# Threshold attention and an ELU feed-forward on one core: held ELUs of two feature-row groups, and a re-ordered early stage

## The chip, the core and the metric

The kernel runs on one core of a Trainium2 chip. Five engines work side by side, each through its own queue in order: TensorE (PE, matmuls, with its weight loads PEld), VectorE (DVE), ScalarE (ACT), GpSimd (POOL) and SyncE (SP, which issues most DMAs). The metric is the device time of one execution in microseconds; lower is better.

## The reference

```python
# attention, batch 8, 8 heads, 576 positions, head size 64, float32
scores = (1/8) * q @ k.T
thresh = max(scores, axis=-1) - tau              # tau = 0.02
attn   = softmax(where(scores >= thresh, scores, -1e9))
x      = (attn @ v), heads side by side          # (8*576, 512)
# feed-forward: 4608 tokens, 512 -> 2048 -> 512
h = x @ w_in
g = where(h > 0, h, exp(min(h, 0)) - 1)          # ELU
out = g @ w_out
```

Everything is float32, outputs included.

## The kernel before

**Attention** goes by pairs of heads: 32 pairs (8 batches of 4), each with four row tiles of 128 queries and a tail of 64. For a tile TensorE computes the scores, VectorE the maximum (`L773`), ScalarE exp of scores less maximum (`L783`), VectorE the mask times exp with its sum (`L787`), VectorE the total and reciprocal (`L545`, `L551`), GpSimd or ScalarE the normalization (`L501`, `L426`). The weights are then turned by 32x32 transposes on VectorE (`L640`) and a round trip through DRAM (`there`), or in part on TensorE, and multiplied by V (`L818`, `L826`). The result is copied to `xt`; the 64 tail tokens of each batch go through DRAM (`xtail`, `L845`) and form a ninth token group.

**Feed-forward** goes by nine groups of 512 tokens. Group 0 is computed plainly. Groups 1 to 8 use a fast matrix scheme with seven products instead of eight. A *first product* (`first_product(g, u)`, `L1444`) makes the hidden values of feature row u (0 to 7) of group g for two halves c of the tokens. ScalarE and VectorE read its banks (`L1458`, `L1466`), ScalarE takes exp into one of three small buffers `ge`, `ge`, `km` (`L1474`), GpSimd or ScalarE subtracts 1 (`L1484`, `L1486`), and VectorE finishes with `min(e - 1, 0) max h`, the ELU (`L1494`). A *second round* multiplies by `w_out`: rounds r = 0 and 1 take feature rows 0 to 3 and 4 to 7. Up to group 6 this is `second_round` (`L1584`). For the last two groups (7 and 8) it is a *deep round*: seven products, some of which are split once more into seven small ones (`deep_product`, matmuls at `L1958`; plain products at `L2020`). A deep round asks VectorE for sums of g into `s_of` before it (`L1864`, `L1866`, queued in `extra` when the second of two feature rows is finished), for second-level sums within it (`kT` and GpSimd's `wTb`, `wTa`, `L1893`), and for adds of what comes out of the banks (`L1970`, `L1980`, `L2026`).

The end of the program runs in this order: first products of group 7, deep round 0 of group 7, first products 0 to 3 of group 8, deep round 1 of group 7, first products 4 to 7 of group 8, deep rounds 0 and 1 of group 8. So the ELUs of the last feature row before a deep round (rows (7,7), (8,3) and (8,7)) aren't needed by that deep round: the one of (7,7) is first read in deep round 1 of group 7, that of (8,3) in deep round 0 of group 8.

**What sets the order.** Three means:

- The early stage (setup, batch 0 and the pairs 4 to 8, group 0 of the feed-forward, the conversion of the weights) is a list of 1270 entries, `EARLY`, written out by hand or by a planner. `follow` walks it: a name is a job (`sc.3` scores of step 3, `su.3` its total, `put.4.2` a copy of turned weights, `rest.7` a weight conversion, `bnorm.5.0.1` a normalization of the pairs, and so on); `:act`, `:dve` or `:pool` picks the engine where it isn't the default; `@f0` picks a bank; `idle17` puts 17 empty transposes on TensorE.
- The steady loop and the end work with an agenda: TensorE's slots advance a clock by a cost, and each piece of work for the other engines is pushed with a due time `at(t, f, key)`; it is issued when the clock passes it. Named shifts move due times: `MOVED` for keys of all even (`s`) or odd (`f`) pairs, `FIRST` for one place.
- `exp(c)` in `first_product` pushes its ELU with a due time; a product that needs it earlier forces all agenda entries up to it. Reusing a `ge` buffer forces the ELU that still reads it. For three feature rows in a set `patient` the due time is 7.0 later once the deep rounds are near:

```python
patient = {(B - 1, 7), (B, 3), (B, 7)}
at(now[0] + (2.0 if c and attending[0] else 1.4)
   + (7.0 if deep_sums and (g, u) in patient else 0.0), lambda: elu(c), f"e{v}{c}")
```

B is 8. All deep and first products together use eight banks in rotation at the end of the program, three at a time.

Of the kernel before, what the change touches and what calls it, by code (L numbers as in the profile page):

```python
# [65 lines left out]
max.1.0 norm.0.0 ld.vd.0.1 prep.q.3.0 first.k.2.0@f0 max.1.1 ld.v.1.1 exp.1.0 th.1.0 rest.1:pool ld.q.3.0
first.t.q.0@f2 exp.1.1 part.0.0@t mask.1.0 th.1.1 add.0 first.k.3.0@f1 prep.k.2.0 mask.1.1 first.t.q.1@f0 ld.v.0.0
su.1:act copy.q.0 sc.2 end.0 norm.0.1:act rec.1 shift.2 prep.k.3.0 norm.1.1 part.0.1@f2 max.2.0 sign.1 idle21@f1
rest.2:pool ld.v.0.1 max.2.1 exp.2.0 th.2.0 ld.vd.0.0 th.2.1 exp.2.1 mask.2.0 add.1 lw.4 put.0.0 mask.2.1 sign.2
norm.1.0 end.1 rest.3 sc.3 ld.v.1.0 su.2:act copy.q.1 add.2 put.0.1 lw.5 part.0.2@t turn.0 max.3.0 part.1.0@f1  # L70
ld.vd.2.1 put.0.2 landed.0 first.q.0.1@f0 max.3.1 exp.3.0 th.3.0 ld.v.3.1 first.q.1.1@f2 part.1.1@t rec.2 ld.v.2.1
th.3.1 exp.3.1 mask.3.0 norm.2.0 ld.vd.1.1 prep.q.0.1 mask.3.1 ld.vd.1.0 put.1.1 part.1.2@f0 turn.1 put.1.0 shift.3
sc.4 end.2 add.3 sign.3 ld.vd.2.0 put.1.2 landed.1 prep.q.1.1 su.3 max.4.0 val.0.block.0@t lw.6 rec.3 max.4.1 exp.4.0
th.4.0 norm.2.1 first.q.2.1@f0 exp.4.1 mask.4.0 th.4.1 part.2.0@f1 norm.3.0 ld.v.2.0 norm.3.1:act idle7@f2 mask.4.1
ld.vd.3.1 put.2.0 end.3 sc.5 su.4:act out.0.block.0 rest.4 shift.4 lw.7 shift.5 sign.4 add.4 ld.v.3.0 max.5.0
part.2.1@t prep.q.2.1 part.2.2@f1 turn.2 val.1.block.0@f2 max.5.1 exp.5.0 th.5.0 rec.4 th.5.1 exp.5.1 mask.5.0
norm.4.0 part.3.0@f0 put.2.2 put.2.1 landed.2 mask.5.1 norm.4.1 part.3.1@f1 put.3.0 part.3.2@t turn.3 rest.5:pool
out.1.block.0 su.5 sc.6 end.4 put.3.1 sign.5 add.5 lw.8 put.3.2 landed.3 max.6.0 val.2.block.0@f0 rest.6 max.6.1
exp.6.0 th.6.0 shift.6 th.6.1 exp.6.1 part.4.0@t mask.6.0 add.6 first.q.3.1@f1 put.4.0 part.4.1@f2 mask.6.1 prep.q.3.1
part.4.2@t turn.4 sign.6 end.5 put.4.2 sc.7 put.4.1 landed.4 rec.5 end.6 lw.9 norm.5.1:act norm.5.0:act  # L80
out.2.block.0:dve val.3.block.0@t su.6 max.7.0 lw.10 max.7.1 th.7.0 exp.7.0 rest.8:pool rec.6 part.5.0@f0
out.3.block.0:dve rest.7 mask.7.0 th.7.1 part.5.1@t norm.6.1 exp.7.1 part.5.2@f1 turn.5 val.0.block.1@f2 shift.8
norm.6.0:act mask.7.1 put.5.0 put.5.2 su.7 sc.8 put.5.1 landed.5 rec.7 shift.7 norm.7.1 sign.8 norm.7.0:act
val.1.block.1@t max.8.0 add.7 max.8.1 exp.8.0 th.8.0 out.0.block.1:dve part.7.0@f0 out.1.block.1 th.8.1 mask.8.0
exp.8.1 add.8 part.6.0@t part.7.1@f1 put.7.0 mask.8.1 part.6.1@f2 sign.7 part.7.2@f0 turn.7 su.8 put.6.0 sc.9 end.7
# [5 lines left out]
norm.10.0 fexp.0.0.0 val.2.block.1@t max.11.0 max.11.1 exp.11.0 th.11.0 fmin.0.0.0 exp.11.1 out.2.block.1:dve
part.10.0@f0 th.11.1 mask.11.0 add.11 part.9.0@t put.10.0 part.9.1@f2 mask.11.1 sign.11 part.10.1@f0 turn.10 shift.12
end.11 sc.12 put.10.1 landed.10 rest.12 shift.13 lw.15 sign.12 su.11:act add.12 half.4@f0 max.12.0 put.9.0 rec.11
max.12.1 exp.12.0 th.12.0 end.12 th.12.1 rest.13 part.9.2@t turn.9 half.5 exp.12.1 mask.12.0 add.13 lw.16 put.9.2
load.q.4 put.9.1 landed.9 mask.12.1 sign.13 sc.13 elu.0.0.0 norm.11.1:act su.12 rec.12 val.0.1@t norm.12.0:act
norm.12.1 max.13.0 end.13 exp.13.0 th.13.0 fexp.0.1.0 mask.13.0 norm.11.0:act fmin.0.1.0 turn.12 su.13:act rest.14
in.0.0:pool sc.14 rest.15 in.0.1:pool rec.13 send.12 in.0.2:pool part.11.0@f1 max.14.0 half.8@f2 in.1.0:pool max.14.1
exp.14.0 th.14.0 elu.0.1.0 th.14.1 lw.17 out.0.1 put.11.0 shift.15 part.11.1@f0 shift.14 exp.14.1 part.11.2@t turn.11
half.2@f1 add.14 mask.14.0 sign.14 put.11.1 mask.14.1 landed.12 norm.13.0:act end.14 sc.15 shift.16 lw.18 put.11.2:dve
landed.11 part.13.0@f0 max.15.0 half.3 max.15.1 exp.15.0 th.15.0 add.15 su.14 sign.15 rec.14 mask.15.0 rest.16 th.15.1  # L100
part.13.1@t turn.13 end.15 exp.15.1 add.16 sc.16 put.13.0 prep.q.4 put.13.1 landed.13 half.9 sign.16 mask.15.1
load.q.5 in.1.1:pool norm.14.1:act max.16.0 in.1.2:pool su.15:act shift.17 val.1.1@t exp.16.0 th.16.0 in.2.0:pool
prep.k.4 fexp.0.0.1 insend.0 rest.18:pool norm.14.0:act mask.16.0 lw.19 rest.17 end.16 fmin.0.0.1:act add.17 su.16
rec.15 lw.20 shift.18 sc.17 out.1.1 rec.16 elu.0.0.1 norm.15.1:act norm.15.0 fexp.0.0.2 part.14.0@t max.17.1 norm.16.0
half.6@f0 put.14.0 max.17.0 in.2.1:pool fmin.0.0.2:act turn.15 exp.17.0 th.17.0 th.17.1 part.14.1@t add.18 sign.17
# [71 lines left out]
def kernel(  # L177
# [13 lines left out]
    B, H, S, D = q.shape  # L191
# [1188 lines left out]
    with tc.manual_schedule():  # L1380
# [748 lines left out]
```

## Time and profile before

| | us |
|---|---|
| median of 3 runs (1269.47 to 1270.43) | 1270.01 |
| the profiled execution | 1268.97 |
| its span, first to last instruction | 1266.9 |

| engine | busy us | share of the span |
|---|---|---|
| PE | 1249.4 | 99% |
| DVE | 1066.1 | 84% |
| POOL | 790.1 | 62% |
| ACT | 584.1 | 46% |

The profile is of one execution, so its sums are made against 1268.97 and not against the median. A timeline row gives start, length, engine, source line, operation, output <- inputs, shape and count, and in brackets idle time in front of it with what ended it. Neighbouring instructions of one line are merged in a row. Lengths overlap by the latency at the end of an instruction, so the distance from start to start is what an instruction costs a busy engine. A row of the chain of waits gives start, length and the engine and line that the end of the program hangs on at that moment; an engine with a q behind its name (SPq) is its sequencer, issuing. The granted TensorE clock was 0.999 in this execution.

### The profile page before, as it was taken

The numbers are of one execution on the slowest core, as the hardware profiler recorded it, in microseconds if no ns is written. First come the engines' busy times: TensorE is split into PE (matmuls) and PEld (weight loads), VectorE is DVE, ScalarE is ACT, GpSimd is POOL, SyncE is SP. The second block draws the span as 40 slices with busy tenths as digits, with TensorE's granted clock in tenths as the row PEclk, the third lists the DMA queues.
The fourth block names the chain that finished last, engine by engine and source line by source line (L and its number), as shares of the span: only waits on it lengthen the run. The fifth ranks groups of instructions, "written<-read, shape, count | busy, mean of one in ns | idle before, by whom it ended". The sixth has DMA issues, their size and how long they took to land.

```text
span 1266.9 us, 22594 instructions
## 1 busy us (share of the span) xinstructions
PE 1249.4 (99%) x7163; PEld 992.5 (78%) x7163; DVE 1066.1 (84%) x2330; ACT 584.1 (46%) x1271; POOL 790.1 (62%) x1144
## 2 busy tenths in 40 slices
PE   7999999999999999999999999999999999999998
PEld 6776576478788887878788878878887888888898
DVE  6998989898889979898889888988989776776776
ACT  6986755453444435352625353443535251434130
POOL 5674544586576747684767657675757474775564
PEclk9999999999999999999999999999999999999999
DMA  9568898998889887988889897988898876334433
GB/s 224 144 177 237 228 260 240 246 299 214 258 205 279 216 245 213 269 238 245 234 226 264 219 267 204 268 214 253 207 279 222 243 217 241 137 125 150 135 112 113
DMA packets 332871, 277.70 MB, mean 219 GB/s; under 512 B 201296, under 2 KB 288336, under 8 KB 332752
## 3 DMA queue, kind: packets, MB, share of 16 engines
q1 hardware_dynamic: 331760, 275.73, 77.9%
q8 instruction: 57, 0.93, 0.3%
q10 hardware_dynamic: 992, 0.53, 0.2%
q14 instruction: 62, 0.51, 0.1%
HBM read 178.85 MB, written 97.32 MB: 218 GB/s over the span
## 4 chain that ended last, share of the span: by engine, by line
PE 79%; DVE 3%; issue 0%; SPq 0%; ACT 0%; DMA 0%; POOL 0%; DVEq 0%; ACTq 0%
PE f L1444 31%; PE f L1584 23%; PE sc L766 8%; PE sc L826 8%; PE f L1958 4%; PE f L2020 2%; PE sc L818 1%; PE sc L813 1%; PE f L953 1%; DVE mx L773 0%; DVE x L640 0%; DVE w_one L787 0%; DMA there<-x 0%; DVE kT L1893 0%; DVE s L1866 0%
## 5 line engine op out<-in xcount | busy, mean ns | idle before, releaser
L773 DVE TENSOR_REDUCE mx<-sc 128x1 f32<-128x576 f32 x252 | 179.9, 750 | 35.5 <-PE sc L766 28.4
L783 ACT ACTIVATE w_one<-sc,mx 128x576 f32<-128x576 f32 x140 | 101.1, 739 | 125.6 <-DVE mx L773 104.5
L779 POOL TENSOR_SCALAR th<-mx,ntau 128x2 f32<-128x2 f32 (+1 forms) x140 | 41.7, 298 | 174.5 <-DVE mx L773 174.4
L766 PE MATMUL sc<-kT,qT 64*128 64x256 f32 (+5 forms) x896 | 126.6, 418 | 2.1 <-ACT xt L432 0.9
L766 PEld LDWEIGHTS sc<-kT,qT 64*128 64x128 f32 x896 | 99.3, 186 | 35.4 <-issue 18.9
L1444 PE MATMUL f<-xt,sw 128*128 128x256 f32 x512 | 123.8, 384 | 0.5 <-ACT xt L432 0.5
L1444 PE MATMUL f<-x,w_in_sb 128*128 128x256 f32 x512 | 122.8, 382 | 0.0
L1444 PE MATMUL f<-xt,w_in_sb 128*128 128x256 f32 x512 | 121.2, 379 | 0.5 <-DVE xt L1053 0.5
L787 DVE SCALAR_TENSOR_TENSOR w_one<-sc,th,w_one 128x576 f32<-128x576 f32 x140 | 109.7, 811 | 13.1 <-ACT w_one L783 12.9
L783 ACT ACTIVATE e<-sc,mx 128x576 f32<-128x576 f32 x112 | 82.7, 742 | 74.5 <-DVE mx L773 72.2
L640 DVE STREAM_TRANSPOSE x<-w_one 128x512 f32<-128x512 f32 (+1 forms) x140 | 100.0, 744 | 15.2 <-POOL w_one L501 10.2
L501 POOL TENSOR_SCALAR w_one<-w_one,rs 128x576 f32<-128x576 f32 x115 | 89.3, 787 | 37.3 <-DVE rs L551 37.3
L1444 PEld LDWEIGHTS f<-xt,sw 128*128 128x128 f32 x512 | 94.1, 190 | 19.5 <-issue 4.3
L1444 PEld LDWEIGHTS f<-x,w_in_sb 128*128 128x128 f32 x512 | 96.2, 190 | 16.1 <-ACT g L1505 3.6
L1444 PEld LDWEIGHTS f<-xt,w_in_sb 128*128 128x128 f32 x512 | 97.2, 190 | 14.0 <-ACT e L783 0.8
L787 DVE SCALAR_TENSOR_TENSOR e<-sc,th,e 128x576 f32<-128x576 f32 x112 | 87.8, 809 | 8.2 <-ACT e L783 7.9
L1584 PE MATMUL f<-w_out_sb,g 128*128 128x256 f32 x384 | 92.0, 382 | 0.0
L1584 PE MATMUL f<-w_out_sb,s 128*128 128x256 f32 x384 | 91.9, 382 | 0.0
L1584 PE MATMUL f<-t,s 128*128 128x256 f32 x384 | 90.7, 379 | 0.0
L501 POOL TENSOR_SCALAR e<-e,rs 128x576 f32<-128x576 f32 x92 | 67.7, 741 | 35.4 <-DVE rs L551 32.6
L1584 PEld LDWEIGHTS f<-w_out_sb,g 128*128 128x128 f32 x384 | 72.0, 190 | 12.2 <-issue 2.9
L1584 PEld LDWEIGHTS f<-w_out_sb,s 128*128 128x128 f32 x384 | 72.0, 190 | 11.8 <-issue 2.5
(344 smaller groups left out, 2902.7 us busy)
## 6 DMA issues: line engine op xcount, KB each, us to landing
there<-x SPq DMA_DIRECT2D x452, 144.0 KB, 3.9
wTb<-there SPq DMA_DIRECT2D x58, 576.0 KB, 6.2
wTa<-there SPq DMA_DIRECT2D x55, 576.0 KB, 4.8
sw<-win_sums SPq DMA_DIRECT2D x62, 384.0 KB, 4.3
t<-wout_sums SPq DMA_DIRECT2D x45, 512.0 KB, 5.2
there<-x SPq DMA_DIRECT2D x112, 80.0 KB, 1.9
wTb<-there SPq DMA_DIRECT2D x56, 160.0 KB, 3.6
wst<-in_moe_w_in_dram SPq DMA_DIRECT2D x16, 512.0 KB, 4.6
```

Source lines behind the costliest of these rows:

```text
L501: nc.gpsimd.tensor_scalar(wv, wv, st["rs"][:, h : h + 1], 1.0, ALU.mult, ALU.mult)
L640: nc.vector.transpose(x[:, :, c0 : c0 + nc_], src.rearrange("p (c g n) -> p g c n", c=nc_, n=T))
L766: on_banks(nc.tensor.matmul(o, qT[r, i * P : (i + 1) * P], kT[r, k0 : k0 + n], start=True, stop=True, skip_group_check=True), o)
L773: on_banks(nc.vector.tensor_reduce(st["mx"][:, h : h + 1], st["sc", h], axis=AX.XY if i == NC else AX.X, op=ALU.max, negate=True), st["sc" ...
L779: nc.gpsimd.tensor_scalar(st["th"][:, cs], st["mx"][:, cs], -1.0, ntau, ALU.mult, ALU.add)
L783: on_banks(nc.scalar.activation(st["e", h], st["sc", h], AF.Exp, bias=st["mx"][:, h : h + 1]), st["sc", h])
L787: on_banks(nc.vector.scalar_tensor_tensor(st["e", h], st["sc", h], st["th"][:, h : h + 1], st["e", h], ALU.is_ge, ALU.mult, accum_out=st[" ...
L826: on_banks(nc.tensor.matmul(o, vm[:, h, c], parts[part][:, g0:g1, h * (NC + 1) + c], start=False, stop=(c == NC - 1), skip_group_check=Tru ...
L1444: nc.tensor.matmul(loc["banks"][place], left[:, j], right[:, j], start=(begins and j == 0), stop=(j == 1), skip_group_check=True)
L1584: nc.tensor.matmul(place(m), lhs, rhs, start=(begins and v == 0), stop=(v == RU - 1), skip_group_check=True)
L1958: nc.tensor.matmul(loc["x"][place][:, :P], left[:, v], right[:, v], start=(begins and v == 0), stop=(v == 1), skip_group_check=True)
L2020: nc.tensor.matmul(loc[c][:, :HM], lefts(g, r, c, m)[:, v], rights(r, m)[:, v], start=(v == 0), stop=(v == RU - 1), skip_group_check=True)
```

## The change

1. **Held ELUs.** `patient` becomes a table of delays: the ELUs of feature rows (7,7) and (8,3) are due 20.0 later instead of 7.0; (8,7) stays at 7.0. In the order that results, the two ELUs (c = 0 and 1) of (7,7), and the four sums of g behind them, leave the middle of deep round 0 of group 7 and stand behind its last adds, among the weight sums (`L1748`) and first adds of group 8's first product. Those of (8,3) leave the middle of deep round 1 and stand at its end and in first product (8,4). Only VectorE's order changes there; those of the other four engines stay.
2. **Early order.** `EARLY` holds the same 1270 entries; some 260 of the jobs stand a few places elsewhere. 24 jobs change engine:

| from, to | jobs |
|---|---|
| DVE to ACT | totals su.0, su.5, su.16, su.19, bsu.4.4, bsu.4.1, bsu.5.4; copy out.2.block.0 |
| ACT to DVE | copy put.4.2 |
| POOL to ACT | rest.0, rest.29, scale.4, bnorm.5.0.1, bnorm.7.2.0 |
| ACT to POOL | rest.7, rest.16, rest.30, rest.31, norm.11.1, bnorm.6.4.0, bnorm.7.1.1 |
| between DVE and POOL | in.4.1 and in.5.2 to POOL, in.4.2 to DVE |

   On ScalarE's queue the first load of K now stands ahead of that of tau. On SP, the xtail stores of some pairs and some fetches stand behind the next send. TensorE's order is unchanged.
3. **Due times.** Nine entries of `MOVED` and one of `FIRST`. In the steady loop this gives VectorE swaps of neighbours (a bank read `L1466` before or after an ELU), the tail's transposes after two of four maxima instead of after all four, and the turn of the next K (`L440`) ahead of the fourth maximum; ScalarE moves a bank copy (`L1506`) behind an exp, GpSimd an add ahead of a subtraction. In pair 9 the fetch of tile 0 is issued 3.6 earlier.

```diff
 FIRST = {
-    "9:3.0": 0.61, "9:turn4": 2.44, ...
+    "9:3.0": 0.61, "9:fetch0": -3.6, "9:turn4": 2.44, ...
 MOVED = {
-    "f20.1": 2.47, "f26.1": 0.42, "f5.1": 4.32, "fout1": 0.83,
-    "s21.0": 0.22, "sexp11": -0.09, "sfetch4": 0.31, "sprep1": -0.32, "sturn4": -1.49,
+    "f20.1": 3.18, "f26.1": -0.14, "f5.1": 3.93, "fout1": 0.47,
+    "s21.0": 0.51, "sexp11": -0.16, "sfetch4": -0.76, "sprep1": -2.36, "sturn4": -3.1,
...
 EARLY = """
-ld.tail.1.0 ld.tau.0.0:act ld.k.0.1 ld.k.0.0:act idle17@f0 ld.q.0.0 ld.k.1.0 ld.k.1.1 lw.0 lw.1 tau first.t.k.0@f0
+ld.tail.1.0 ld.k.0.0:act ld.k.0.1 ld.tau.0.0:act idle17@f0 ld.q.0.0 ld.k.1.1 ld.k.1.0 lw.0 lw.1 first.t.k.0@f0
...
-put.7.1 end.8 lw.11 rest.9 half.0@f1 rec.8 load.k.4 shift.9 put.6.1 max.9.0 add.9 norm.8.1:act put.7.2:dve landed.7
...
+half.0@f1 shift.9 load.k.4 put.6.0 rec.8 max.9.0 add.9 norm.8.1:act put.7.2:dve landed.7 exp.9.0 max.9.1 part.6.2@t
...
-        patient = {(B - 1, 7), (B, 3), (B, 7)}
+        patient = {(B - 1, 7): 20.0, (B, 3): 20.0, (B, 7): 7.0}
...
-                at(now[0] + (2.0 if c and attending[0] else 1.4) + (7.0 if deep_sums and (g, u) in patient else 0.0), lambda: elu(c), f"e{v}{c}")
+                at(now[0] + (2.0 if c and attending[0] else 1.4) + (patient.get((g, u), 0.0) if deep_sums else 0.0), lambda: elu(c), f"e{v}{c}")
```

More of the change, by code (lines that the diff above doesn't have):

```diff
@@ L66 @@
[L66 to L85, printed above, removed]
@@ L91 @@
[L91 to L105, printed above, removed]
@@ new lines @@
+ld.v.0.1 exp.2.0 th.2.0 rest.2:pool ld.vd.0.0 exp.2.1 mask.2.0 th.2.1 add.1 put.0.0 lw.4 mask.2.1 sign.2 rest.3
+norm.1.0 sc.3 end.1 ld.v.1.0 su.2:act copy.q.1 put.0.1 add.2 part.0.2@t turn.0 lw.5 max.3.0 part.1.0@f1 put.0.2
+landed.0 ld.vd.2.1 first.q.0.1@f0 max.3.1 exp.3.0 ld.v.3.1 first.q.1.1@f2 th.3.0 rec.2 part.1.1@t th.3.1 exp.3.1
+ld.v.2.1 mask.3.0 norm.2.0 ld.vd.1.1 prep.q.0.1 mask.3.1 put.1.1 ld.vd.1.0 part.1.2@f0 turn.1 put.1.0 shift.3 sc.4
+end.2 add.3 sign.3 ld.vd.2.0 put.1.2 landed.1 prep.q.1.1 su.3 val.0.block.0@t max.4.0 lw.6 rec.3 max.4.1 exp.4.0
@@ new lines @@
+th.4.0 norm.2.1 first.q.2.1@f0 exp.4.1 mask.4.0 part.2.0@f1 th.4.1 norm.3.0 idle7@f2 ld.vd.3.1 norm.3.1:act mask.4.1
+ld.v.2.0 put.2.0 end.3 sc.5 su.4:act out.0.block.0 rest.4 shift.4 lw.7 shift.5 sign.4 add.4 ld.v.3.0 part.2.1@t
+max.5.0 prep.q.2.1 part.2.2@f1 turn.2 val.1.block.0@f2 max.5.1 exp.5.0 th.5.0 rec.4 th.5.1 exp.5.1 mask.5.0 norm.4.0
+part.3.0@f0 put.2.2 put.2.1 landed.2 mask.5.1 part.3.1@f1 norm.4.1 put.3.0 part.3.2@t turn.3 end.4 out.1.block.0
+rest.5:pool sc.6 su.5:act put.3.1 sign.5 lw.8 add.5 val.2.block.0@f0 max.6.0 put.3.2 landed.3 rest.6 max.6.1 shift.6
@@ new lines @@
+exp.6.0 th.6.0 part.4.0@t rec.5 th.6.1 exp.6.1 mask.6.0 first.q.3.1@f1 add.6 part.4.1@f2 put.4.0 mask.6.1 prep.q.3.1
+part.4.2@t turn.4 sign.6 end.5 sc.7 put.4.1 put.4.2:dve landed.4 lw.9 end.6 norm.5.1:act val.3.block.0@t max.7.0
+out.2.block.0 lw.10 norm.5.0:act su.6 max.7.1 th.7.0 exp.7.0 part.5.0@f0 out.3.block.0:dve th.7.1 exp.7.1 mask.7.0
+rest.7:pool part.5.1@t part.5.2@f1 turn.5 val.0.block.1@f2 rec.6 mask.7.1 norm.6.1 norm.6.0:act put.5.0 shift.8
+rest.8:pool put.5.2 sc.8 su.7 put.5.1 landed.5 rec.7 shift.7 sign.8 add.7 val.1.block.1@t norm.7.0:act max.8.0 max.8.1
@@ new lines @@
+half.1 exp.10.0 th.10.0 rec.9 put.8.0 put.8.2 lw.13 put.8.1 mask.10.0 norm.9.0 landed.8 end.10 norm.9.1 su.10:act
+first.t.q.3@f2 first.t.q.2@f0 sc.11 copy.q.2 copy.q.3 shift.11 rest.11 lw.14 rec.10 val.2.block.1@t fexp.0.0.0
+norm.10.0 max.11.0 max.11.1 exp.11.0 th.11.0 fmin.0.0.0 part.10.0@f0 out.2.block.1:dve exp.11.1 mask.11.0 th.11.1
+part.9.0@t add.11 put.10.0 part.9.1@f2 mask.11.1 sign.11 part.10.1@f0 turn.10 shift.12 sc.12 put.10.1 landed.10 end.11
+rest.12 shift.13 sign.12 lw.15 add.12 half.4@f0 max.12.0 su.11:act put.9.0 max.12.1 exp.12.0 th.12.0 rec.11 end.12
@@ new lines @@
+th.12.1 rest.13 part.9.2@t turn.9 half.5 mask.12.0 exp.12.1 lw.16 add.13 load.q.4 put.9.2 put.9.1 landed.9 mask.12.1
+sign.13 sc.13 elu.0.0.0 norm.11.1 su.12 val.0.1@t rec.12 max.13.0 norm.12.0:act norm.12.1 end.13 exp.13.0 th.13.0
+fexp.0.1.0 mask.13.0 norm.11.0:act fmin.0.1.0 turn.12 su.13:act rest.14 in.0.0:pool sc.14 rest.15 in.0.1:pool rec.13
+send.12 part.11.0@f1 max.14.0 in.0.2:pool half.8@f2 max.14.1 in.1.0:pool exp.14.0 elu.0.1.0 th.14.0 th.14.1 lw.17
+out.0.1 put.11.0 shift.15 part.11.1@f0 shift.14 exp.14.1 part.11.2@t turn.11 half.2@f1 add.14 mask.14.0 sign.14
@@ new lines @@
+put.17.1 sign.21 part.19.1@t turn.19 in.5.0 add.22 part.17.2@f1 turn.17 half.12@f2 put.19.1 landed.19 end.21 put.17.2
+landed.17 in.5.1 in.5.2:pool val.3.1@t shift.23 insend.5 sign.23 insend.4 rest.23 lw.25 sign.22 add.23 copy.k.4:act
+end.22 prep.k.5 rest.24:pool lw.26 out.3.1 t tail.4 half.19 bmax.4.4.0 insend.2 shift.24 bexp.4.4.0 bth.4.4 add.24
+sign.24 bmask.4.4.0 idle3@f1 end.23 bsu.4.4:act wsc.4.0.0 brec.4.4 end.24 lw.27 bnorm.4.4.0:act wsc.4.0.1 insend.3
+shift.25 rest.25 lw.28 bmax.4.0.0 half.16@f1 insend.1 bmax.4.0.1 bexp.4.0.0 load.q.6 bturn.4.4 bth.4.0 sign.25
```

147 lines of the change are left out of this document (76 added, 71 removed), and 18 rows, old and new, of the table MOVED.

## The prediction

> **What bounds the kernel now.** I read the page's busy line first, then the windows, then TensorE's timeline where a window shows it short of full, and last VectorE's and GpSimd's timelines beside those places.
>
> ```profile
> PE 1249.4 (99%) x7163; PEld 992.5 (78%) x7163; DVE 1066.1 (84%) x2330; ACT 584.1 (46%) x1271; POOL 790.1 (62%) x1144
> ```
>
> ```profile
> 0.00:40.00 40.00, 33.59 (x252) 25.61 (x253) 28.28 (x68) 30.20 (x63) 23.64 (x50) 1.00 0.87 205
> 40.00:80.00 40.00, 38.97 (x329) 30.78 (x328) 36.79 (x89) 38.14 (x79) 25.43 (x37) 1.00 0.56 150
> ...
> 440.00:480.00 40.00, 40.00 (x227) 32.31 (x226) 32.64 (x72) 15.78 (x35) 19.97 (x32) 1.00 0.89 248
> ...
> 1120.19:1143.40 23.21, 21.93 (x161) 20.44 (x160) 19.02 (x42) 5.02 (x15) 16.44 (x17) 1.00 0.34 114
> 1217.18:1238.38 21.20, 21.20 (x162) 20.30 (x160) 16.15 (x41) 5.03 (x15) 11.90 (x14) 1.00 0.42 141
> ```
>
> In a window row, the columns behind the length are busy time of TensorE, its weight loads, VectorE, ScalarE and GpSimd. TensorE is the bound: 1249.4 us of 1266.9. In the steady loop (440 to 480) it is busy 40.00 of 40, so nothing that changes there can save time; it can only lose some. What can be won lies where TensorE stands still: in the early stage (the first two rows) and in the deep rounds. The last two rows are the first and the third deep round, group 7 round 0 and group 8 round 0. They issue the same slots of matmuls, yet the one takes 23.21 us and the other 21.20, without a gap. The first loses 2.01 us to waits.
>
> **Deep round 0 of group 7.** The four gaps in TensorE's timeline, and two rows of the chain of waits that give the undisturbed pace (0.44 to 0.45 us for four 128x128 instructions, so 0.89 for eight, 1.73 for eight 128x256):
>
> ```profile
> 1131.62 0.61 PE L1958 MATMUL f<-t,g 128*128 128x128 f32 x4
> 1133.23 1.16 PE L1958 MATMUL f<-x,kT 128*128 128x128 f32 x8 [1.00 <-DVE kT L1893]
> 1134.23 1.89 PE L2020 MATMUL f<-w_out_sb,s 128*128 128x256 f32 x8
> 1136.16 0.68 PE L1958 MATMUL f<-x,wTb 128*128 128x128 f32 x4
> ...
> 1139.80 0.61 PE L1958 MATMUL f<-w_out_sb,s 128*128 128x128 f32 x4
> 1140.65 1.13 PE L1958 MATMUL f<-w_one,kT 128*128 128x128 f32 x8 [0.24 <-issue]
> ```
>
> ```profile
> 1189.65 1.73 PE f L2020 x8
> 1191.38 0.44 PE f L1958 x4
> ```
>
> Start to start, less the pace: 1131.62 to 1133.23 is 1.61 - 0.45 = 1.16 lost; then 1.00 - 0.89 = 0.11; 1.93 - 1.73 = 0.20; and 1139.80 to 1140.65 is 0.85 - 0.45 = 0.40. Together 1.87 of the 2.01. The largest ends on VectorE's kT (the second-level sums, L1893). What VectorE did before it:
>
> ```profile
> 1128.52 1.64 DVE L1494 SCALAR_TENSOR_TENSOR wTb<-km,wTb 128x512 f32<-128x512 f32 x1
> ...
> 1130.60 0.97 DVE L1866 TENSOR_TENSOR s<-wTb 128x256 f32<-128x256 f32 x1
> 1131.49 0.41 DVE L1893 TENSOR_TENSOR kT<-g 128x256 f32<-128x256 f32 x1
> 1131.83 0.41 DVE L1864 TENSOR_TENSOR e<-s,wTb 128x256 f32<-128x256 f32 x1
> 1132.16 0.68 DVE L1494 SCALAR_TENSOR_TENSOR wTa<-ge,wTa 128x512 f32<-128x512 f32 x1
> 1132.77 0.41 DVE L1893 TENSOR_TENSOR kT<-kT,g 128x256 f32<-128x256 f32 x1
> ...
> 1133.70 0.94 DVE L1866 TENSOR_TENSOR qm<-wTa 128x256 f32<-128x256 f32 x1
> ...
> 1134.97 0.55 DVE L1864 TENSOR_TENSOR e<-qm,wTa 128x256 f32<-128x256 f32 x1
> ```
>
> The two L1494 rows are the held ELUs, the L1866 and L1864 rows the sums of g that follow them. The change takes all six out of the round and leaves the rest of VectorE's order as it is. Ahead of the end of kT that is 1.64 + 0.89 + 0.34 + 0.61 (start to start from the second on) = 3.48 us; kT was complete at 1132.77 + 0.41 = 1133.18, and would be at about 1129.7. TensorE wants it at 1131.62 + 0.45 = 1132.07. The gap of 1.16 closes, and 0.11 and 0.20 with it, since VectorE then has no backlog (0.94 and 0.55 more go behind it). I don't count the 0.40: by VectorE's rows around it the sum in front of TensorE is held up there by other things than the backlog. Taken: 1.47; ends: 0 and 2.01.
>
> What speaks against it is GpSimd, which runs two long sums at the same time:
>
> ```profile
> 1128.34 2.95 POOL L1051 TENSOR_TENSOR x<-xt 128x512 f32<-128x512 f32 x2
> ```
>
> The ELU that starts inside this row takes 1.64, the one at 1132.16, outside it, 0.68. So 0.96 of the first ELU is a wait on GpSimd, and the kT sums that move up may inherit it. At worst the first kT sum runs only between GpSimd's two sums and the second after 1128.34 + 2.95 = 1131.29, hence ready at 1131.29 + 0.41 = 1131.70, still 0.37 ahead of 1132.07. The Trainium skill (SBUF — State Buffer, Who interferes with whom) says that a VectorE instruction with both inputs in SBUF and a GpSimd instruction that reads SBUF take a shared port in turns, each for its whole length. By that rule the 0.96 is not removed with the ELU but passes to the next such VectorE instruction, which is kT; passed on in full to TensorE it would leave 3.0 - 0.96 = 2.0 us of the sum below, 1268.0. The trace agrees with it in 1.64 against 0.68, and rival (b) has its chance from there.
>
> **Deep round 1 of group 7**, where the ELUs of group 8's first four feature rows go out:
>
> ```profile
> 1180.35 0.61 PE L1958 MATMUL f<-t,wTb 128*128 128x128 f32 x4
> 1181.53 1.16 PE L1958 MATMUL f<-x,kT 128*128 128x128 f32 x8 [0.57 <-DVE kT L1893]
> 1182.52 1.89 PE L2020 MATMUL f<-w_out_sb,qm 128*128 128x256 f32 x8
> 1184.57 0.68 PE L1958 MATMUL f<-x,wTb 128*128 128x128 f32 x4 [0.15 <-POOL ot L1906]
> 1185.09 1.89 PE L2020 MATMUL f<-t,vm 128*128 128x256 f32 x8
> ```
>
> ```profile
> 1177.24 0.68 DVE L1494 SCALAR_TENSOR_TENSOR g<-ge,g 128x512 f32<-128x512 f32 x1
> ...
> 1178.37 0.96 DVE L1866 TENSOR_TENSOR s<-g 128x256 f32<-128x256 f32 x1
> ...
> 1180.12 0.41 DVE L1864 TENSOR_TENSOR s<-s,g 128x256 f32<-128x256 f32 x1
> 1180.46 0.68 DVE L1494 SCALAR_TENSOR_TENSOR g<-km,g 128x512 f32<-128x512 f32 x1
> ```
>
> Lost: 1.18 - 0.45 = 0.73, 0.99 - 0.89 = 0.10, 2.05 - 1.73 = 0.32, 0.52 - 0.45 = 0.07; 1.22 together. The four rows ahead of the kT sum come to 0.68 + 0.96 + 0.41 + 0.68 = 2.73, more than any of the gaps. The 0.32 ends on GpSimd's ot, which adds up what VectorE wrote, and goes with it. Taken: 1.22; ends: 0 and 1.22.
>
> **What the six instructions cost where they go.** They now stand at the head of the next four first products:
>
> ```profile
> 1150.47 0.42 DVE L1466 TENSOR_TENSOR g<-f,t 128x256 f32<-128x256 f32 x1 [1.42 <-POOL t L1463]
> ...
> 1198.79 0.42 DVE L1466 TENSOR_TENSOR wTb<-f,t 128x256 f32<-128x256 f32 x1 [3.56 <-POOL t L1463]
> ```
>
> At the undisturbed durations they are 2 x 0.68 + 4 x 0.41 = 3.00 us, at round 0's 5.19. VectorE idles 1.42 and 3.56 us there. Behind them queue the remaining reads of the deep round's banks, the weight sums (L1748), then the first add. The first add of group 8 may come up to 3.8 us late. ScalarE's exp and GpSimd's minus wait for it, TensorE does not: its eight banks go round in more than two products of three banks, each 28 instructions of 256 columns or 3.5 x 1.73 = 6.1 us long, and nobody reads the g in question before the next deep round (gaps near 1180 above; 1217.18 for the second group). Cost taken: 0; if that cover were gone, up to 3.8.
>
> **The steady loop.** Besides swaps of neighbours, the turn of the next K (L440) goes ahead of the fourth maximum in 11 pairs:
>
> ```profile
> 449.29 0.77 DVE L440 STREAM_TRANSPOSE kT<-qm 128x576 f32<-128x576 f32 x1
> ...
> 451.27 0.81 DVE L787 SCALAR_TENSOR_TENSOR w_one<-sc,th,w_one 128x576 f32<-128x576 f32 x1
> ...
> 456.73 0.45 PE L813 MATMUL sc<-kT,qT 64*64 64x288 f32 x1
> ```
>
> The maximum, its exp and so the last mask can come 0.77 later; the mask ends at 452.08, TensorE needs the banks at 456.73: 4.65 us of cover. Cost 0; without cover 0.77 in each of 11 pairs, 8.5 us.
>
> **The early order.** TensorE's own order is the same instruction for instruction; the 24 jobs that change engine and the others that move shift only who feeds it. Seven totals go from VectorE to ScalarE, and SP issues one send ahead of an xtail store (its issue is in the chain of waits):
>
> ```profile
> 13.67 0.15 DVE L545 TENSOR_REDUCE su<-sm 128x2 f32<-128x4 f32 x1
> ```
>
> ```profile
> 17.35 0.30 ACT L512 ACTIVATE su<-sm 128x2 f32<-128x2 f32 x1 [0.56 <-DVE w L537]
> ```
>
> ```profile
> 230.06 0.44 SPq L845
> ```
>
> Best: 7 x 0.15 + 0.44 = 1.5 us won, all on the path. Worst: 7 x 0.30 = 2.1 us lost, all on ScalarE, which is busy 38.14 of 40 in the second window. I take 0.3 won: nearer to the middle, on the side of the better end, because in that window ScalarE gives up a normalization, a conversion and a small copy and gets one total and one copy.
>
> **Sum.** 1.47 + 1.22 + 0.3 + 0 + 0 = 3.0 us. The profiled execution took 1268.97 (span 1266.9 and 2.07 around it) and would take 1266.0. The median of the runs is 1270.01, 1.04 above it, so the forecast for it is 1267.0.
>
> **Rivals.**
> (a) The early order pays in full and the 0.40 and the rest of round 0 go too: 2.01 + 1.22 + 1.5 = 4.7 won, 1265.3. For it: round 2 of the trace runs without a gap even with its ELUs inside. Against: every early term would have to lie on the path.
> (b) The kT sums of round 0 take over the whole wait on GpSimd, and TensorE still stops near 1133: round 1's 1.22 alone, 1268.8. For it: 0.96 of the ELU is that wait already. Against: 0.37 us to spare at the worst alternation.
> (c) The early order loses its 2.1 on ScalarE: 2.7 - 2.1 = 0.6 won, 1269.4.
> (d) Slower: the turn of K ahead of the fourth maximum delays the tail scores in all 11 pairs: 8.5 - 3.0 = 5.5 lost, 1275.5. It decides once the last mask is later by more than 4.65 us; the shift is 0.77.
> That the ELUs come back into the round by a forced read is excluded: in the new order they stand behind the round's last sums.
>
> **How the numbers follow.** Forecast 0.55, (a) 0.13, (b) 0.22, (c) 0.06, (d) 0.04. Under 0.2%, 2.5 us, a measurement of this kernel can hardly tell from no change. Of the forecast's 0.55 I put 0.44 beyond 2.5 us; with (a) faster is 0.57. The other 0.11, (b) and five sixths of (c) are within: 0.38. (d) and the rest: 0.05. The range, 1265.2 to 1269.4, reaches from (a) to (c) and leaves out (d) and the ends.
>
> **What would show it.** Right: the window from the first L2020 of group 7 to the next L1444 falls from 23.21 to 21.2 to 21.8, no TensorE row there with a gap ending on kT; round 1 without the 0.73; both held ELUs at about 0.7 us behind it. Wrong: a gap of about 1 us still in front of f<-x,kT (b); a TensorE busy time below 40.00 in a steady window (d); a later first L2020 than 1120.19 by over a microsecond (c).

## Result and the profile after

| | before | after |
|---|---|---|
| median (6 runs each) | 1269.71 us | 1265.07 us |
| lowest to highest | 1269.14 to 1270.43 | 1264.75 to 1266.22 |
| profiled execution | 1268.97 | 1265.16 |
| its span | 1266.9 | 1263.4 |

The ratio is 0.9966, with a 95% interval of 0.9955 to 0.9978: 2.8 to 5.7 us faster, 4.6 by the medians. The forecast was 1267.0. The measured median lies 0.1 below the range's lower end of 1265.2.

The busy line and the windows of after. The last two windows are deep rounds 0 and 1 of group 7, from the first L2020 to the next L1444.

```profile
PE 1247.3 (99%) x7163; PEld 992.0 (79%) x7163; DVE 1067.8 (85%) x2322; ACT 584.5 (46%) x1276; POOL 787.2 (62%) x1147
```

```profile
0.00:40.00 40.00, 33.88 (x256) 25.76 (x258) 29.98 (x71) 32.51 (x68) 23.50 (x49) 1.00 0.80 208
40.00:80.00 40.00, 39.27 (x332) 31.02 (x333) 36.68 (x86) 35.94 (x75) 27.50 (x39) 1.00 0.59 156
...
1119.46:1140.68 21.22, 21.22 (x162) 20.39 (x161) 15.40 (x36) 5.03 (x15) 15.05 (x17) 1.00 0.37 125
1166.19:1187.72 21.53, 21.53 (x150) 20.29 (x149) 19.18 (x50) 1.15 (x2) 13.47 (x17) 1.00 0.31 99
```

Round 0 fell from 23.21 to 21.22 us and round 1 from 22.74 (1168.92 to 1191.66) to 21.53. TensorE is busy in all of both. That is 1.99 + 1.21 = 3.2 us. VectorE has 3.6 us less to do in the window of round 0, 15.40 in place of 19.02. Round 0 in TensorE's timeline of after:

```profile
1130.89 0.61 PE L1958 MATMUL f<-t,g 128*128 128x128 f32 x4
1131.34 1.06 PE L1958 MATMUL f<-x,kT 128*128 128x128 f32 x8
1132.23 1.89 PE L2020 MATMUL f<-w_out_sb,s 128*128 128x256 f32 x8
1133.96 0.61 PE L1958 MATMUL f<-x,wTb 128*128 128x128 f32 x4
...
1137.53 0.61 PE L1958 MATMUL f<-w_out_sb,s 128*128 128x128 f32 x4
1137.98 1.07 PE L1958 MATMUL f<-w_one,kT 128*128 128x128 f32 x8
```

From row to row it is 0.45, 0.89, 1.73 and 0.45 us, the undisturbed pace in every case. All four gaps are gone, the one of 0.40 too that the prediction did not count. VectorE in after, and GpSimd's long sums beside it:

```profile
1128.35 0.29 DVE L1980 TENSOR_TENSOR ot<-f,wTb 128x128 f32<-128x128 f32 x1
1128.56 0.59 DVE L1893 TENSOR_TENSOR kT<-g 128x256 f32<-128x256 f32 x1
1129.26 1.30 DVE L1893 TENSOR_TENSOR kT<-kT,g 128x256 f32<-128x256 f32 x1
...
1135.94 0.47 DVE L1893 TENSOR_TENSOR kT<-s 128x256 f32<-128x256 f32 x1
1136.52 1.31 DVE L1893 TENSOR_TENSOR kT<-kT,s 128x256 f32<-128x256 f32 x1
...
1141.51 0.68 DVE L1494 SCALAR_TENSOR_TENSOR wTb<-km,wTb 128x512 f32<-128x512 f32 x1
...
1142.45 0.68 DVE L1494 SCALAR_TENSOR_TENSOR wTa<-ge,wTa 128x512 f32<-128x512 f32 x1
```

```profile
1127.60 2.67 POOL L1051 TENSOR_TENSOR x<-xt 128x512 f32<-128x512 f32 x2
```

The held ELUs run behind the round at 0.68 each. The kT sums moved up to where the ELUs were and took over their wait on GpSimd: 0.59 and 1.30 in place of 0.41 each. The second is ready at 1130.56, 0.78 us before TensorE wants it (1131.34).

The rest of the difference lies elsewhere. TensorE's 7163 matmuls stand in the same order in both kernels, so the start of each can be compared with that of the same matmul. This table gives by how many us each kernel's TensorE is later than the profiled before (minus: ahead), at points named by the time in before. All rows but the first are kernels told of below.

| | 34 | 157 | 950 | 1101 | last matmul |
|---|---|---|---|---|---|
| after | -1.16 | -1.51 | -1.76 | -0.73 | -3.95 |
| after, second trace | -0.57 | -0.89 | -1.11 | -0.89 | -4.11 |
| early order alone | -0.83 | -1.13 | -1.41 | -1.32 | -1.33 |
| held ELUs alone | -0.10 | 0.47 | 0.62 | 0.64 | -2.58 |
| due times alone | -0.01 | -0.39 | -0.29 | -0.10 | 0.22 |
| early order and held ELUs | -1.16 | -1.46 | -1.74 | -1.66 | -4.88 |
| the same, second trace | -0.44 | -0.76 | -1.05 | -0.98 | -4.21 |

After is ahead by 1.2 us at 34 already, and by 1.8 before 950. Of that it loses 1.0 between 950 and 990, all of it in front of this row of TensorE's timeline of after; before has no idle time there:

```profile
961.40 1.99 PE L1444 MATMUL f<-xt,sw 128*128 128x256 f32 x8 [0.81 <-DMA sw<-win_sums]
```

The lead at 34 begins with the first load of K. The rows of TensorE and of ScalarE's queue in before, and then in after, where tau's load is issued behind that of K:

```profile
1.46 3.89 PE L554 MATMUL f<-ident 128*128 128x128 f32 x17 [1.46 <-POOL ident masks.py:199]
5.28 0.37 PE L405 MATMUL f<-ident,w_out_sb 64*128 64x64 f32 x1
6.03 0.63 PE L554 MATMUL f<-ident,w_out_sb 128*128 128x128 f32 x4 [0.38 <-DMA w_out_sb<-in_k_dram]
...
12.73 1.24 PE L493 MATMUL sc<-x 64*128 64x288 f32 x8 [0.69 <-DVE w L537]
...
19.00 0.66 PE L554 MATMUL f<-ident,w 128*128 128x128 f32 x4 [0.40 <-ACT w L426]
```

```profile
0.74 0.40 ACTq L1125 DMA_DIRECT2D tau_sb<-in_tau_dram  x1
1.19 0.44 ACTq L1125 DMA_DIRECT2D w_out_sb<-in_k_dram  x1
```

```profile
1.46 3.55 PE L554 MATMUL f<-ident 128*128 128x128 f32 x17 [1.46 <-POOL ident masks.py:199]
4.94 0.27 PE L405 MATMUL f<-ident,w_out_sb 64*128 64x64 f32 x1
5.17 0.63 PE L554 MATMUL f<-ident,w_out_sb 128*128 128x128 f32 x4
...
10.87 0.76 PE L554 MATMUL f<-ident 128*128 128x128 f32 x5 [0.46 <-ACT qT L426]
...
11.72 1.24 PE L493 MATMUL sc<-x 64*128 64x288 f32 x8
```

```profile
0.74 0.45 ACTq L1125 DMA_DIRECT2D w_out_sb<-in_k_dram  x1
```

K is issued 0.45 us earlier, and the matmul that waited for it starts 0.86 earlier. Of this 0.34 is not the load: the 17 empty transposes in front are done in 3.55 us in place of 3.89. Their single length falls from 0.42 to 0.27 us within the start, in this execution sooner than in that of before; in the second trace of after the transposes take 3.89 again, and it is 0.46 ahead at that matmul.

The wait on VectorE's w in front of the matmul at 12.73 is gone too, but nearly all of it stands just ahead instead, as a wait on ScalarE's qT (the row at 10.87): the two together bring 0.14 us. The largest step of the other moves is at 19.00 of before, where the wait of 0.40 on ScalarE's w is gone (the same matmul starts at 17.49 in after): 0.64 us together with the row behind it. Of that 0.4 us is lost again in front of the scores at 31.70. From 8 us of before on, when the effect of the start is over, all five traces with the early order gain 0.84 to 0.91 us more up to 950, about a third of it by 34 and a third between 34 and 157. In the three traces with the early order that start as slowly as before (the second of after, the second of the two parts together, the early order alone) the lead at 950 is 1.05 to 1.41 us.

### The profile page after: what moved, and what is told of

It is laid out like the page before. It is cut to its first block, busy times and chain, and to the rows that moved or that the text cites. A ratio compares the mean times of both kernels' runs of the same rounds, so it can differ in the third digit from the quotient of the medians.

```text
span 1263.4 us, 22606 instructions
## 1 busy us (share of the span) xinstructions
PE 1247.3 (99%) x7163; PEld 992.0 (79%) x7163; DVE 1067.8 (85%) x2322; ACT 584.5 (46%) x1276; POOL 787.2 (62%) x1147
## 4 chain that ended last, share of the span: by engine, by line
PE 90%; DVE 4%; DMA 2%; ACT 2%; issue 1%; SPq 0%; POOL 0%; DVEq 0%; ACTq 0%; POOLq 0%
PE f L1444 30%; PE f L1584 23%; PE sc L766 9%; PE sc L826 9%; PE f L1958 4%; PE f L2020 3%; PE f L953 2%; PE f L913 2%; PE sc L493 2%; PE sc L818 1%; PE sc L813 1%; DVE mx L773 1%; PE f L554 1%; PE sc L712 1%; PE f L885 1%
## 5 line engine op out<-in xcount | busy, mean ns | idle before, releaser
L779 POOL TENSOR_SCALAR th<-mx,ntau 128x2 f32<-128x2 f32 (+1 forms) x140 | 46.0, 329 | 189.9 <-DVE mx L773 189.8
L1444 PE MATMUL f<-xt,sw 128*128 128x256 f32 x512 | 123.7, 384 | 1.3 <-DMA sw<-win_sums 0.8
L1444 PE MATMUL f<-x,w_in_sb 128*128 128x256 f32 x512 | 122.8, 382 | 0.0
L1444 PE MATMUL f<-xt,w_in_sb 128*128 128x256 f32 x512 | 121.2, 379 | 0.5 <-DVE xt L1053 0.5
L1444 PEld LDWEIGHTS f<-xt,sw 128*128 128x128 f32 x512 | 94.1, 190 | 20.2 <-issue 4.3
L1444 PEld LDWEIGHTS f<-x,w_in_sb 128*128 128x128 f32 x512 | 96.2, 190 | 16.1 <-ACT g L1505 3.6
L1444 PEld LDWEIGHTS f<-xt,w_in_sb 128*128 128x128 f32 x512 | 97.2, 190 | 14.0 <-ACT e L783 0.8
L1584 PEld LDWEIGHTS f<-t,s 128*128 128x128 f32 x384 | 73.0, 190 | 9.9
```

What stands on the lines that cost most here:

```text
L779: nc.gpsimd.tensor_scalar(st["th"][:, cs], st["mx"][:, cs], -1.0, ntau, ALU.mult, ALU.add)
L1444: nc.tensor.matmul(loc["banks"][place], left[:, j], right[:, j], start=(begins and j == 0), stop=(j == 1), skip_group_check=True)
L1584: nc.tensor.matmul(place(m), lhs, rhs, start=(begins and v == 0), stop=(v == RU - 1), skip_group_check=True)
```

## Experiments

**One part at a time.** Each of the first three is the kernel before with one part of the change; the fourth has two.

```diff
# held ELUs alone
-        patient = {(B - 1, 7), (B, 3), (B, 7)}
+        patient = {(B - 1, 7): 20.0, (B, 3): 20.0, (B, 7): 7.0}
# early order alone: EARLY of after, all else of before
# due times alone: MOVED and FIRST of after, all else of before
# early order and held ELUs: MOVED and FIRST of before, all else of after
```

> The kernel before with the held ELUs alone: (7,7) and (8,3) due 20.0 later, the early order and the due times as before. Theory (the three parts of the change work each for itself): the two traces place 1.99 us of the gain in deep round 0 of group 7 (23.21 to 21.22) and 1.21 in deep round 1 (22.74 to 21.53), so about 3.2 us faster than before, and TensorE has no gap in either round. Rival (the sizes of the prediction): 2.7, with the 0.40 us in front of f<-w_one,kT still there. Rival (the waits of the rounds depend on how the earlier stages leave the engines): less than 2, with some of the gaps in the trace.

> The kernel before with the early order alone. Theory: matched matmul by matmul, TensorE in the changed kernel is 1.35 us ahead by 118 us and keeps that to 600, so 1.35 us faster, with the gaps of the two deep rounds as before (1.2 us in front of f<-x,kT in round 0). Rival (the prediction's term): 0.3 us faster. Rival (TensorE's lead is used up at the next common wait): nothing at the end although the lead is there at 118 us.

> The kernel before with the ten due times alone. Theory A (the load of the sums of w_in is issued late enough to be missed): TensorE waits about 0.8 us for sw near 961 us, as in the changed kernel's trace, and the time is 0.3 to 0.8 us longer than before. Theory B (that wait was one execution's DMA and not the order): no such row, and the time is the same within 0.3 us.

> The early order and the held ELUs together, the due times as before: the changed kernel without its third part. Theory (parts add up): 3.2 + 1.35 = 4.5 us faster than before. If the due times cost the 0.8 us of the wait for sw, this beats the changed kernel by 0.5 to 0.8 us; if they cost nothing, it equals it within 0.3 us; if they gain the 0.3 us by which TensorE's lead grew between 118 and 622 us, it is that much slower.

| beside before at 1269.36 | median | by the medians | ratio, 95% |
|---|---|---|---|
| held ELUs alone | 1266.01 | -3.35 | 0.9974 (0.9963 to 0.9984) |
| early order alone | 1267.70 | -1.66 | 0.9987 (0.9978 to 0.9996) |
| due times alone | 1269.88 | +0.52 | 1.0002 (0.9993 to 1.0011) |
| early order and held ELUs | 1264.12 | -5.24 | 0.9957 (0.9945 to 0.9970) |

Rounds 0 and 1 with the held ELUs alone:

```profile
1120.83:1142.04 21.21, 21.21 (x161) 20.38 (x160) 15.42 (x36) 5.03 (x15) 15.09 (x17) 1.00 0.38 125
1167.56:1189.08 21.52, 21.52 (x149) 20.28 (x148) 19.20 (x50) 1.15 (x2) 13.47 (x17) 1.00 0.31 99
```

They are what they are in after, 2.00 and 1.22 us shorter than before, without the other two parts. So the held ELUs give 3.2 us, whatever the early stage does. The early order alone keeps its lead to the end (-1.33 in the table): nothing later uses it up. The parts add up, 3.35 + 1.66 = 5.0 against 5.24. The due times, the third part, bring nothing; whether they cost something was the next question.

**After and the version without its due times, side by side.**

> The changed kernel once more, beside the kernel without its due times on the same chip. If the 0.81 us that TensorE waited for sw at 960.6 us belongs to the order of the change, its trace shows that row again and it stays 0.6 to 0.9 us behind the kernel without the due times. If it was a transfer that landed late in one execution, the row is gone and the two kernels are within 0.4 us of each other.

> The early order and the held ELUs without the due times, once more, beside the changed kernel on the same chip. If the due times cost something in every execution: 0.6 to 0.9 us faster than the changed kernel. If they do nothing: the same within 0.4 us.

On one chip, after took 1264.99 us (0.9965 of before, 0.9953 to 0.9978) and the version without the due times 1264.31 (0.9958, 0.9945 to 0.9972). The second trace of after has no wait for sw: the row at 961 stands there without idle time, so the 0.81 us was a transfer that landed late in one execution. Neither does the trace of the due times alone have it, while that of a kernel without them (30 in place of 20, below) loses 0.23 in front of the same matmul. What comes back in these two traces with the due times is small: 0.2 us at the scores at 973 us, where the three traces of the early order without them lose 0.07 to 0.09 and the first trace of after, where the wait for sw had delayed TensorE before, loses nothing. Over both chips the ten runs without the due times have a median of 1264.19 (1263.77 to 1265.14) and the eleven runs of after 1264.99 (1264.64 to 1266.22). The kernel without the third part is thus the fastest of all, by 0.7 to 0.8 us by the medians; its ratio's interval overlaps that of after. The place at 973 accounts for 0.1 of it. Where the rest comes from, and whether late landings have a part in it, was not settled.

**What in the early order pays.** Two single edits to the kernel before:

```diff
# the first load of K ahead of tau
-ld.tail.1.0 ld.tau.0.0:act ld.k.0.1 ld.k.0.0:act idle17@f0
+ld.tail.1.0 ld.k.0.0:act ld.k.0.1 ld.tau.0.0:act idle17@f0
# the seven totals on ScalarE: su.0 -> su.0:act, and likewise
# su.5, su.16, su.19, bsu.4.4, bsu.4.1, bsu.5.4
```

> The kernel before with one edit in the early order: on ScalarE's queue the first load of K ahead of that of tau. Theory A (the start is bound by the landing of the first K): TensorE passes 6.03 us of before 0.45 to 0.86 earlier, since the load's issue moves up by 0.45 us (1.19 to 0.74), and what is left at 118 us is between 0.25 and 0.86; time 0.3 to 0.9 us shorter. Theory B (the lead is lost in the next wait on VectorE's w, because tau comes later or VectorE is the bound there): nothing left at 20 us, same time.

> The kernel before with another single edit in the early order: the seven totals su.0, su.5, su.16, su.19, bsu.4.4, bsu.4.1 and bsu.5.4 on ScalarE in place of VectorE. Prediction's price: between 7 x 0.15 = 1.05 us faster and 7 x 0.30 = 2.1 slower. Theory A (VectorE's queue is what TensorE waits for early): 0.3 to 1.05 faster. Theory B (only the order of the jobs pays, not the engine): the same within 0.3 us. Rival (ScalarE is the bound between 40 and 80 us): slower by 0.3 or more.

Beside before at 1269.29, the load of K alone gave 1268.69 (0.9994, 0.9985 to 1.0003) and the totals alone 1269.12 (0.9999, 0.9990 to 1.0008). TensorE with the load of K alone:

```profile
5.34 0.66 PE L554 MATMUL f<-ident,w_out_sb 128*128 128x128 f32 x4
...
11.96 1.24 PE L493 MATMUL sc<-x 64*128 64x288 f32 x8 [0.69 <-DVE w L537]
```

The matmul at 6.03 starts 0.69 us earlier (0.15 of it by the transposes: 5.13 in place of 5.28 for the one in front), and TensorE is 0.60 ahead at the last matmul. The time agrees, -0.6, though its interval holds no change. The waits of 0.69 on w at 11.96 and of 0.40 on ScalarE's w, now at 18.23, stay: those go by other moves of the early order. By the runs the seven totals do nothing that can be measured. Their profiled execution was the slowest of that kernel, 1270.87, and 1.7 us late at the matmul that stands at 9.02 in before, ahead of the first of the totals. Of that 0.96 us stands in this row, which takes 1.24 in the others:

```profile
8.64 2.20 PE L493 MATMUL sc<-x 64*128 64x288 f32 x8
```

From there on the matched matmuls can still be compared. The trace with the totals loses another 0.39 us in front of the scores that stand at 31.70 in before, where VectorE's mask waits for GpSimd's w. The five traces with the early order, which has the same seven totals, lose 0.39 to 0.41 there, and none of the traces without them loses anything. So at that place the totals cost, and the gain of the early order comes in spite of them. In the medians (-0.17) this can't be seen.

**Where the held work comes from and where it lands.** Four variants of the kernel before:

```diff
# (7,7) alone
+        patient = {(B - 1, 7): 20.0, (B, 3): 7.0, (B, 7): 7.0}
# all three
+        patient = {(B - 1, 7): 20.0, (B, 3): 20.0, (B, 7): 20.0}
# 30 in place of 20
+        patient = {(B - 1, 7): 30.0, (B, 3): 30.0, (B, 7): 7.0}
# sums of x later; patient as in before
-                    at(clock[0] + 2.99 * k + 8.0, f, f"x{k}")
+                    at(clock[0] + 2.99 * k + 13.0, f, f"x{k}")
```

> The kernel before with only the ELUs of (7,7) due 20.0 later; those of (8,3) and (8,7) stay at 7.0. Theory (each round's waits come from its own held ELUs): round 0 of group 7 takes 21.2 us in place of 23.21, round 1 keeps its 22.74 with the gaps of 0.73 and 0.32; 2.0 us faster than before. Rival (round 1's gaps follow from round 0's): round 1 falls too, 3.2 us faster.

> All three delays at 20.0: the ELUs of (8,7) too leave deep round 0 of group 8, which has no gap to close, and by the order stand with their four sums right ahead of the kT sums of the last round. There kT is ready at 1241.10 and wanted at 1241.89 in the trace of before, 0.79 to spare; the six instructions are 2 x 0.60 + 4 x 0.34 = 2.6 us start to start. Theory (what counts is where the held work lands, and its cover there): 2.6 - 0.8 = 1.8 us slower than with (7,7) and (8,3) alone, so about 1.4 faster than before. Rival (VectorE idles 0.98 us just ahead and takes them up there): at most 0.8 us slower than with the two alone.

> The kernel before with the sums of x for the last group (L1051 and the rows behind it) due 5.0 later, so that GpSimd's two long sums no longer lie beside the held ELUs, which stay in the round. Theory A (0.96 us of the first ELU's 1.64 is a wait on GpSimd): that ELU takes about 0.7, kT is ready 0.96 earlier and the gap of 1.16 in front of f<-x,kT shrinks to about 0.2; up to 1.0 us faster than before, less what the sums cost in their new place. Theory B (the wait is VectorE's own, the backlog alone): the ELU still takes 1.6 and the gap stays at about 1.16; same time.

> The kernel before with the ELUs of (7,7) and (8,3) due 30.0 later in place of 20.0: they stand further on among the first products of group 8. Theory (the first products have cover for them, nobody reads these g before the next deep round): as with 20.0, 3.2 to 3.5 us faster than before. Rival (the reads of the banks that queue behind them hold TensorE up): slower than with 20.0 by 0.5 or more, with a TensorE gap in a first product of group 8.

| beside before at 1269.10 | median | by the medians | ratio, 95% |
|---|---|---|---|
| (7,7) alone | 1267.10 | -2.00 | 0.9983 (0.9974 to 0.9992) |
| all three | 1268.56 | -0.54 | 0.9996 (0.9987 to 1.0005) |
| 30 in place of 20 | 1266.40 | -2.70 | 0.9977 (0.9969 to 0.9986) |
| sums of x later | 1269.08 | -0.02 | 0.9998 (0.9989 to 1.0007) |

With (7,7) alone round 0 gives its 2.0 us and round 1 keeps its gaps:

```profile
1179.58 1.16 PE L1958 MATMUL f<-x,kT 128*128 128x128 f32 x8 [0.57 <-DVE kT L1893]
...
1182.62 0.68 PE L1958 MATMUL f<-x,wTb 128*128 128x128 f32 x4 [0.15 <-POOL ot L1906]
```

So each round's waits come from its own held ELUs.

With all three held, nearly the whole gain is gone. First TensorE at the start of the last round, then VectorE, then GpSimd, at the same time:

```profile
1238.96 0.61 PE L1958 MATMUL f<-t,e 128*128 128x128 f32 x4
1241.38 1.13 PE L1958 MATMUL f<-x,kT 128*128 128x128 f32 x8 [1.81 <-issue]
```

```profile
1236.18 0.85 DVE L1494 SCALAR_TENSOR_TENSOR wTb<-ge,wTb 128x512 f32<-128x512 f32 x1
1236.95 0.68 DVE L1494 SCALAR_TENSOR_TENSOR wTa<-ge,wTa 128x512 f32<-128x512 f32 x1
1237.55 1.49 DVE L1866 TENSOR_TENSOR s<-wTb 128x256 f32<-128x256 f32 x1
1239.07 0.42 DVE L1864 TENSOR_TENSOR e<-s,wTb 128x256 f32<-128x256 f32 x1
...
1240.86 0.42 DVE L1893 TENSOR_TENSOR kT<-kT,e 128x256 f32<-128x256 f32 x1
```

```profile
1237.11 1.65 POOL L1876 TENSOR_TENSOR vm<-wTb 128x512 f32<-128x512 f32 x1 [0.63 <-DVE wTb L1494]
```

The label "issue" must not mislead: kT ends at 1241.28 and the matmul that reads it begins 0.1 later. From 1238.96 it is 2.42 to the next row, 1.97 more than the pace. Expected was a loss of 1.8; by the medians, each against its own before, it is 2.8 worse than with two held; matched matmul by matmul it loses 2.5 there (2.94 ahead before the last round, 0.44 at the end). The price came out higher since one sum behind the ELUs took 1.49 in place of 0.41: it lasted until GpSimd's sum beside it had ended. Six instructions that cost nothing in front of a first product cost 2.5 us in front of a kT sum.

With 30 in place of 20 the window of the first products that take up the ELUs of (8,3) is full:

```profile
1188.58:1214.09 25.51, 25.51 (x126) 22.62 (x125) 17.05 (x30) 10.44 (x26) 15.74 (x19) 1.00 0.43 134
```

The cover is there. By the medians, each against its own before, this kernel is 0.65 us behind the one with 20, on the rival's side of the 0.5; but the intervals overlap, and the rival's mechanism is not there: matched matmul by matmul 0.2 us is lost in round 1 and 0.3 in deep round 0 of group 8, nothing in a first product. The trace of the due times alone, with the ELUs due as before, loses 0.3 in that round too, so the second loss need not come from the 30.

With the sums of x later and the ELUs left in the round, first VectorE, then TensorE, then GpSimd:

```profile
1128.76 0.68 DVE L1494 SCALAR_TENSOR_TENSOR wTb<-km,wTb 128x512 f32<-128x512 f32 x1
...
1131.49 0.42 DVE L1893 TENSOR_TENSOR kT<-kT,g 128x256 f32<-128x256 f32 x1
...
1134.16 1.48 DVE L1893 TENSOR_TENSOR kT<-vm 128x256 f32<-128x256 f32 x1
```

```profile
1131.86 0.61 PE L1958 MATMUL f<-t,g 128*128 128x128 f32 x4
1132.31 1.06 PE L1958 MATMUL f<-x,kT 128*128 128x128 f32 x8
1133.20 1.89 PE L2020 MATMUL f<-w_out_sb,s 128*128 128x256 f32 x8
1135.94 0.68 PE L1958 MATMUL f<-x,wTb 128*128 128x128 f32 x4 [0.85 <-POOL x L1051]
```

```profile
1133.92 1.44 POOL L1051 TENSOR_TENSOR x<-xt 128x512 f32<-128x512 f32 x1
```

The ELU takes 0.68 in place of 1.64, and the gap of 1.16 is not 0.2 but gone, with four of the six instructions still ahead of kT's end: the wait on GpSimd was the part that made the gap. But the sum stands in front of GpSimd's next work and holds VectorE's next kT for 1.48, and 2.74 - 1.73 = 1.01 us of a gap opens there. Most of the wait was moved, not removed: the round takes 22.30 us in this trace (1120.43 to 1142.73), 0.91 less than before, against 2.0 less with the ELUs held, and 0.2 of that is lost again in deep round 0 of group 8. The runs show nothing of the remaining 0.7: by the medians the time is the same, and the interval reaches from 1.4 us faster to 0.9 slower. Theory A is thus right on the ELU and the gap, and what the change is worth in time stays open. With the ELUs held kT still waits for GpSimd, but there is slack in front of TensorE.

## Why the prediction was right, and where it was off

The sign and the main mechanism were right; the size was 3.0 of 4.6. What came about is close to rival (a), 4.7 us and 1265.3, which had a chance of 0.13: round 0 in full, and the early order paying far more than the 0.3 taken. But (a) made its 1.5 us for the early order of the totals, which bring nothing by the medians, and of one issue on SP, which was not tested alone; that its size comes near the measured one is luck.

- **Round 0, 1.47: mis-sized by the gap left out.** The chain (four of the six instructions less in front of kT's end, ready well before it is wanted) held; measured 1.99 to 2.01. The step that failed is that the 0.40 in front of `f<-w_one,kT` was "held up there by other things than the backlog". VectorE's rows of before in front of it:

```profile
1138.03 0.28 DVE L1980 TENSOR_TENSOR wTb<-f,wTb 128x128 f32<-128x128 f32 x1
1138.23 0.91 DVE L1893 TENSOR_TENSOR kT<-s 128x256 f32<-128x256 f32 x1
1139.25 1.30 DVE L1893 TENSOR_TENSOR kT<-kT,s 128x256 f32<-128x256 f32 x1
```

  There is no idle time before 1138.23: VectorE was still working off the backlog. In after the same pair starts at 1135.94, waits as long on GpSimd (1.31), and is ready at 1137.83 for a matmul at 1137.98. The last row does wait on GpSimd, but being late was due to the backlog.
- **Round 1, 1.22: right**, 1.21 in after, 1.22 with the held ELUs alone.
- **The wait on GpSimd, rival (b): the mechanism was right and the cover held.** The wait passed to kT, 0.18 + 0.89 = 1.07 us, with 0.78 to spare where the prediction had worked out 0.37. The rule of the Trainium skill (SBUF — State Buffer, Who interferes with whom) that the two engines take turns for whole instructions agrees with these rows; the 2.0 us that the prediction worked out by it did not come, because the wait ended ahead of the matmul.
- **New place, 0: right.** TensorE has no gap in the first products; with all three held, where the cover was gone, the same six instructions cost 2.5 us.
- **Steady loop, 0: right in kind.** The turn of K ahead of the fourth maximum costs nothing that shows: in the trace of the due times alone TensorE loses 0.10 us from 157 to 950, where that of the held ELUs alone loses 0.15. At 973 us the due times lose about 0.1, and one execution had a late landing of 0.81, a DMA that the prediction didn't look at. Beside the kernel without them after is 0.7 to 0.8 slower by the medians, and most of that is unexplained.
- **Early order, 0.3: the term that was mis-sized most.** Measured 1.66 alone by the medians, 1.33 in the matched trace. The bounds were made of the seven totals and one issue on SP. The totals bring nothing by the medians, and in the traces they cost 0.4 at one place. The load of K, which the diff shows and the prediction did not price, is worth about 0.5: 0.60 by the medians, 0.69 - 0.15 in the trace. Its price could be read off before's rows: TensorE idle on that load at 6.03, its issue 0.45 behind tau's. The other moves bring the rest, 0.84 to 0.91 in the matched traces. Which of them do was not taken apart; the wait on ScalarE's w at 19.00 is the place where it shows most (with the load of K alone it stays, with the whole order it is gone).
- **The base.** The forecast put the profiled execution 1.04 below the median of 1270.01. With six runs the median is 1269.71 and after's profiled execution lies on its median: 0.3 of the 4.9 us between 1270.01 and 1265.07 is the base.

## What to carry to other kernels

Work that nobody needs soon belongs where its queue has slack, and the same work put right in front of a tight dependency costs what goes beyond the slack there (2.5 us here): look up for each held instruction what stands behind it at the new place and when that is wanted. When a gap ends on an engine, read back along that engine to its last idle time; everything since then is one backlog, and the gaps fed by it can close together, as the four of round 0 did. In an early stage price the first loads first: a load that TensorE waits for, issued behind one that it doesn't need yet, is worth about the issue time in between (0.45 us here; 0.46 to 0.54 in the traces).

## What the runs showed of the hardware beyond what was expected

- VectorE sums of 128x256 that met a GpSimd sum ended 0.28 to 0.29 us after it did: kT in after, 1130.56 against 1130.27; kT with the sums of x later, 1135.64 against 1135.36; the sum at 1237.55 with all three held, 1239.04 against 1238.76. Undisturbed they take 0.41. It looks like a full block until the other's end, not a slower pace. Adds that read a bank kept their 0.29 us inside the same GpSimd sum (1128.35 in after).
- TensorE starts at about half its pace and comes up to it at a time that varies from execution to execution: a 128x128 transpose takes 0.42 us at first and 0.27 later, from start to start 0.21 and 0.11, a change that falls near 4.5 us in after, between 5 and 6 in before, and after 9 in the trace with the totals (2.20 for the scores in place of 1.24). The two traces of after stand 0.6 apart at 34 us because of it, and the trace with the totals is 1.7 late at the matmul at 9.02. The granted clock shows 1.00 in these stretches of before, of after and of the kernel with the totals, and does not tell it. The Trainium skill (TensorE: Matmul & The Clock Gate, What's actually happening) says that the array's clock begins throttled and is released by a window of activity that runs freely, so that the same kernel warms up at another moment each time; these rows agree. Half a microsecond between two single profiles is no finding here unless the start is taken out by matching matmuls.
